# Attention and two feed-forward blocks on one core: plain float32 scores for batch 0, and a Float64 conversion that shifts on ScalarE

## The chip, the cores and the metric

The program runs on one core of a Trainium2 chip. The metric is the device time of one execution in microseconds (us). Five engines work side by side, each on its own queue, in order: TensorE (PE, with its weight loads as PEld), VectorE (DVE), ScalarE (ACT), GpSimd (POOL) and SyncE (SP), which here only issues DMAs.

## The reference

Attention with rotary embedding over 4 batches, 8 heads, 576 positions, 64 features; then a layer norm with a two-layer feed-forward block (512 to 2048 to 512) and a residual; then a gated block with a causal convolution of 5 taps.

```python
q_rot, k_rot = rotate(q), rotate(k)
scores = scale * q_rot @ k_rot.T
attn = softmax(scores)
x = attn @ v                                  # (4, 576, 512) after the heads are joined
xn = layer_norm(x) * g_ln
x = x + relu(xn @ w_ch1) @ w_ch2
gate = sigmoid(causal_conv5(x, conv_w))
out = (gate * (x @ w_val)) @ w_out
```

The weights arrive as Float64 and are converted on the chip.

## The kernel before

**Order.** Every piece of work is a step with an engine, an assumed duration, a rank, the steps that it waits for and the buffers that it takes. A planner (class `Plan`) plays these steps through once while the program is built and so fixes the order in which each engine gets its instructions. On the chip each engine takes them strictly in that order. A changed duration or dependency can therefore move work anywhere in the program.

**Attention.** A part is a batch and a pair of heads (and, in batches 0 and 1, a range of rows of q). For each part SP loads k (576 columns) and q (`load`); DVE multiplies by the rotary table (`mul`, L308) and adds the two halves (`add`, L312). Then the rotated value is split: ACT rounds it to float32r, the reduced float32 that TensorE takes in one pass (`hi`, L326), and DVE writes the remainder (`lo`, L330). A score tile has 128 rows by 576 columns in two halves of 288; `a_scores` (L443) adds three products of halves (high by high, high by low, low by high). Two heads sit in the two halves of the partitions and go as a pair: 12 matmuls. A last tile per part (its "lead", with the 64 left-over rows of both heads put in a block-diagonal `qd`) takes 6. Behind a score tile come the row maximum (DVE, L448), the exponential (ACT, L454), a split into two float16 (ACT L460, DVE L465), a transposing DMA to `pT`, and the products with v (PE, L489 and L492). Two score tiles fit in PSUM at a time. Batch 0 has 16 pairs and 4 leads; its k lies in `kx0`, which batch 1 uses again.

**Weights.** Each of 16 blocks of `w_ch1` and `w_ch2` (1024 columns of Float64, 1 MB) is loaded, then turned into float32 by `Conv`: ACT makes the upper bits from the upper word (`p1`, L586), DVE shifts the result left by 3 (L590) and then ors in the lower word, shifted right by 29 (L591; both in `p2`). PE forms a bound of the column norms (L607); from it come scales, and the float32 block is split into two float16 (ACT L645, DVE L648). The first feed-forward product (L745, `f1`) needs the blocks of `w_ch1`; the second (L773, `f2`) those of `w_ch2`, which are split last.

**Tail.** The gated block works on pairs of row tiles, nine in all: the residual output (DVE L777), a byte shuffle (DVE L868), a transposing DMA, a copy back (DVE L880), a float32r split (ACT L888, DVE L893), the gate (DVE L908 among others), four groups of value products (PE L921, 12 matmuls each), the product with the gate and its split (DVE L926, ACT L932, DVE L936), and two groups of output products (PE L948, 12 each).

Of the kernel before, what the change touches and what calls it, by code (L numbers as in the profile page):

```python
# [11 lines left out]
I32 = mybir.dt.int32  # L12
ACTF = mybir.ActivationFunctionType
# [140 lines left out]
def kernel(ctx: ExitStack, tc: tile.TileContext, qk, v, g_ln, w_ch1, w_ch2, w_val, conv_w, w_out, rope, eye, out):  # L154
    nc = tc.nc
# [19 lines left out]
    plan = Plan(dict(raw0=RAW, raw=RAW, qx=2, qs=QS, kx0=1, kx1=1, kx2=1, kx3=1, kq=KQ, qd=1, vt0=2, vt=1, vh=NP, sv=4, vb=2, vm=2, ss=2, so=1, nmx=4, p32=2, p16=P16, pT=PT,  # L175
# [16 lines left out]

    kx0 = xpool.tile([128, NP, 2, S], F32R, name="kx0", tag="x1")
# [44 lines left out]
    c_q = plan.step(POOL, 0.4, -999, lambda: nc.gpsimd.memset(qd.bitcast(F32), 0.0))  # L238
# [48 lines left out]
    def plan_prep(p):  # L287
# [17 lines left out]
        def mul(n):  # L305
            a = st["r", n]
            t = (rope_sb[:, :, q0:q1], rope_sb)[n]
            nc.vector.tensor_tensor(out=a, in0=a, in1=t, op=ALU.mult)  # L308

        def add(n):  # L310
            a = st["r", n]
            nc.vector.tensor_tensor(out=a[:, 0], in0=a[:, 0], in1=a[:, 1], op=ALU.add)  # L312

        def hi(n):
# [4 lines left out]
            elif n:  # L319
                st["x"][1] = kx0[:, pr]  # L320
            elif p >= NP:
                st["x"][0] = ap_q.tile([128, 2, QX], F32R, name="qs", tag="qs", bufs=QS)[:, :, 0:nq]
                st["x"][1] = prep[base[p]]["x"][1]
            else:
                st["x"][0] = pool.tile([128, 2, nq], F32R, name="qx", tag="qx", bufs=2)
# [6 lines left out]
        def diag():  # L332
            c = ts[0][1] - q0
            for h in range(2):
                sl = slice(64 * h, 64 * h + 64)
                nc.scalar.copy(out=qd[sl, :, sl], in_=st["x"][0].bitcast(F32)[sl, :, c:c + 64])

        ready = [bufs[base[p]]["k"]] if two else []
        for n in ((0,) if two else (1, 0)):
# [5 lines left out]
            x = plan.step(DVE, dve(w), r, lambda n=n: add(n), after=[x], uses=[bf["raw", n]])  # L345
            takes = []
            if n:
                takes = [Buf("kq" if b > 1 else f"kx{pr}")]
                bf["kq"] = takes[0]
            elif b < 2:  # L350
                takes = [Buf("qs" if p >= NP else "qx")]
                bf["q"] = takes[0]
            else:
                bf["q"] = bf["kq"]
            uses = [bf["raw", n]] + ([bf["q"]] if not n and not takes else [])
# [16 lines left out]
        if ts[0][0] is None:  # L372
            bf["qd"] = Buf("qd")
# [55 lines left out]
    def a_scores(i):  # L429
# [4 lines left out]
        if h is None:  # L434
            todo = [(slice(0, 128), qd)]
# [93 lines left out]
    for i in range(NS):  # L529
# [3 lines left out]
        if h != 1:  # L533
            ne = 1 if h is None else 2
            ss = [Buf("ss") for _ in range(ne)]
            x = plan.step(PE, 0.85 if h is None else 1.08, R_SC + i, lambda i=i: a_scores(i), after=bf["ready"] + ([bf["dg"]] if h is None else []), takes=ss,
# [4 lines left out]
            if b < 2:  # L541
# [42 lines left out]

# [469 lines left out]
```

## Time and profile before

| | |
|---|---|
| median of 3 runs | 786.35 us (785.13 to 787.8) |
| the profiled execution | 786.84 us |
| its span, first to last instruction | 785.0 us |
| PE, DVE, ACT busy | 88%, 82%, 56% of the span |
| mean granted clock of TensorE | 0.948 of 2.4 GHz |

The difference between the profiled execution and its span, 1.84 us, lies around the program. Shares over the whole span are averages over stages with different limits, so the stages are read one by one below.

### The profile page before, as it was taken

Reading aid. Unit: us, or ns where it says so; the run is one execution under the profiler, and the core shown is the slowest. Engines: PE = TensorE matmul, PEld = TensorE weight load, DVE = VectorE, ACT = ScalarE, POOL = GpSimd, SP = SyncE. Lnnn points to the kernel's source line nnn. Section 1 sums busy time; section 2 is a strip of 40 time slices with the busy share of each in tenths; the row PEclk is TensorE's granted clock in tenths of the full one; section 3 lists DMA queues with packets and bytes.
Section 4 is the critical chain, followed back from the end, with each engine's and each line's share of the span. In section 5 each row is a group of like instructions: output and inputs, shape, how many; then the busy total and the mean of one; then the engine's idle time right before and its main releaser. Section 6 shows DMA issues by size and latency. Waiting matters only on the chain.

```text
span 785.0 us, 19308 instructions
## 1 busy us (share of the span) xinstructions
PE 688.6 (88%) x8001; PEld 541.5 (69%) x8001; DVE 640.5 (82%) x1302; ACT 440.8 (56%) x773; POOL 16.4 (2%) x39
## 2 busy tenths in 40 slices
PE   1344868868999999999999999999999999999967
PEld 1233757744678776767687878777787888888746
DVE  6989989999989999997899978677799997664225
ACT  5755655787776556776767666554444443343113
POOL 0000000000000000000000000000000000000000
PEclk9985877778999999999999999999999999999988
DMA  8996489855888898788789687657424321010100
GB/s 308 247 313 141 79 215 281 188 129 133 127 144 145 169 186 163 135 162 170 125 163 179 110 137 128 114 109 217 85 52 81 54 68 42 28 41 29 41 14 28
DMA packets 231736, 103.62 MB, mean 132 GB/s; under 512 B 210784, under 2 KB 218976, under 8 KB 231648
## 3 DMA queue, kind: packets, MB, share of 16 engines
q1 hardware_dynamic: 231648, 102.39, 61.4%
q8 instruction: 63, 1.03, 0.5%
q14 instruction: 25, 0.20, 0.1%
HBM read 45.73 MB, written 4.72 MB: 64 GB/s over the span
## 4 chain that ended last, share of the span: by engine, by line
PE 58%; DVE 23%; DMA 10%; ACT 5%; issue 4%; SPq 0%; ACTq 0%; DVEq 0%
PE acc L773 17%; PE hp L745 16%; DMA pT<-p 8%; PE po L948 6%; PE sc L443 6%; PE pv L921 5%; PE ov L489 4%; DVE p L465 3%; DVE nmx L448 3%; DVE raw L308 2%; DVE gt L908 2%; PE ov L492 2%; DVE wall L648 2%; ACT p L454 1%; DMA raw<-in_qk_dram 1%
## 5 line engine op out<-in xcount | busy, mean ns | idle before, releaser
L745 PE MATMUL hp<-xT,wall 128*128 128x128 f16 x3456 | 209.6, 222 | 2.2 <-DVE wall L648 2.2
L745 PEld LDWEIGHTS <-wall 128*128 128x128 f16 x3456 | 199.4, 99 | 7.2 <-DVE wall L648 2.5
L773 PE MATMUL acc<-wall,hh 128*128 128x512 f16 x544 | 162.9, 381 | 0.0
L454 ACT ACTIVATE p<-sc,nmx 128x576 f32<-128x576 f32 x144 | 105.3, 735 | 87.5 <-DVE nmx L448 86.4
L465 DVE SCALAR_TENSOR_TENSOR p<-p,p 128x576 f16<-128x576 f32 x144 | 107.2, 752 | 22.4 <-ACT p L460 21.4
L489 PE MATMUL ov<-vh,pT 128*128 128x65 f16 (+1 forms) x1296 | 97.4, 203 | 29.2 <-DMA pT<-p 23.0
L489 PEld LDWEIGHTS <-pT 128*128 128x128 f16 x1296 | 81.2, 101 | 47.2 <-DMA pT<-p 32.7
L448 DVE TENSOR_REDUCE nmx<-sc 128x1 f32<-128x576 f32 x144 | 104.8, 748 | 3.1 <-PE sc L443 3.0
L773 PE MATMUL acc<-wall,hl 128*128 128x512 f16 x272 | 103.4, 380 | 0.0
L460 ACT ACTIVATE p<-p 128x576 f16<-128x576 f32 x144 | 97.4, 681 | 4.4 <-DMA pT<-p 1.6
L773 PEld LDWEIGHTS <-hh 128*128 128x128 f16 x544 | 48.9, 98 | 50.9 <-issue 2.2
L908 DVE SCALAR_TENSOR_TENSOR gt<-xT,cw,gt 128x256 f32<-128x256 f32 (+4 forms) x192 | 72.1, 413 | 5.5 <-ACT gt L899 2.9
L763 DVE SCALAR_TENSOR_TENSOR hl<-hp,hh 128x512 f16<-128x512 f32 x68 | 46.6, 685 | 30.9 <-ACT hh L757 30.9
L492 PE MATMUL ov<-vl,pT 128*128 128x64 f16 (+1 forms) x720 | 71.0, 203 | 0.0
L757 ACT ACTIVATE hh<-hp 128x512 f16<-128x512 f32 x68 | 40.2, 591 | 45.6 <-PE hp L745 45.2
L492 PEld LDWEIGHTS <-pT 128*128 128x128 f16 x720 | 54.8, 102 | 3.4
L921 PE MATMUL pv<-xh,wvh 128*128 128x256 f32 x144 | 45.2, 314 | 6.5 <-ACT xh L888 6.5
L308 DVE TENSOR_TENSOR raw<-raw,rope_sb 128x1152 f32<-128x1152 f32 (+2 forms) x56 | 46.8, 835 | 3.6 <-DMA raw<-in_qk_dram 3.6
L773 PEld LDWEIGHTS <-hl 128*128 128x128 f16 x272 | 26.7, 98 | 32.6 <-issue 0.6
L443 PE MATMUL sc<-kx,qs 64*128 64x288 f32 x336 | 38.2, 344 | 12.0 <-ACT p L454 12.0
L948 PE MATMUL po<-woh,gv 128*128 128x512 f32 x144 | 47.3, 399 | 0.4 <-DVE gv L936 0.4
L921 PE MATMUL pv<-xl,wvh 128*128 128x256 f32 x144 | 41.8, 290 | 1.1 <-DVE xl L893 1.1
(118 smaller groups left out, 944.4 us busy)
## 6 DMA issues: line engine op xcount, KB each, us to landing
raw<-in_qk_dram SPq DMA_DIRECT2D x24, 576.0 KB, 4.5
wall<-in_moe_w_ch_dram SPq DMA_DIRECT2D x8, 1024.0 KB, 6.2
kk<-in_moe_w_ch_dram SPq DMA_DIRECT2D x8, 1024.0 KB, 6.1
vt<-in_v_dram SPq DMA_DIRECT2D x16, 320.0 KB, 3.2
out_dram<-x SPq DMA_DIRECT2D x18, 256.0 KB, 2.0
raw<-in_qk_dram SPq DMA_DIRECT2D x24, 128.0 KB, 2.8
pT<-p SPq DMA_TRANSPOSE x144, 3.4
r<-in_moe_w_val_dram SPq DMA_DIRECT2D x4, 512.0 KB, 4.9
```

The source lines that it names most:

```text
L443: nc.tensor.matmul(live[i + e][:, half, 0:HS], lw[rows, a], xk[rows, k, half * HS:(half + 1) * HS], start=(n == 0), stop=(n == 2))
L448: nc.vector.tensor_reduce(out=nmx, in_=sc[:, :, 0:HS], axis=AX.XY, op=ALU.max, negate=True)
L454: nc.scalar.activation(out=p32.rearrange("p (e n) -> p e n", e=2), in_=sc[:, :, 0:HS], func=ACTF.Exp, bias=nmx)
L460: nc.scalar.activation(out=p16[:, 0], in_=p32, func=ACTF.Copy, scale=P_SCALE)
L465: nc.vector.scalar_tensor_tensor(out=p16[:, 1], in0=p32, scalar=P_SCALE, in1=p16[:, 0], op0=ALU.mult, op1=ALU.subtract)
L489: nc.tensor.matmul(o, pT[:, c], vh[:, 2 * c + hs:2 * c + hs + nh], start=(c == 0), stop=(c == 8))
L492: nc.tensor.matmul(o[..., 0:D], pT[:, c], vl[:, 2 * c + hs:2 * c + hs + nh], start=False, stop=False)
L745: nc.tensor.matmul(hp[:, j], w1[:, u, wl * 512 + o:wl * 512 + o + 128], xT[:, xl * KD + c], start=(i == 0), stop=(i == 3 * KD - 1))
L773: nc.tensor.matmul(st["acc"], lw[:, j], w2[:, f + j, lo * 512:lo * 512 + 512], start=(f + j == 0 and i == 0), stop=(f + j == KF - 1 and i ...
L908: nc.vector.scalar_tensor_tensor(out=gt[:, c0:c1], in0=xT[:, c, HALO + c0 - s:HALO + c1 - s], scalar=col(KT - 1 - s, c), in1=gt[:, c0:c1], ...
L921: nc.tensor.matmul(pv, lw[:, d, c * 128:(c + 1) * 128], rx[:, d], start=(n == 0), stop=(n == 3 * KD - 1))
L948: nc.tensor.matmul(po, lw[:, d, sl], rx[:, d, :], start=(n == 0), stop=(n == 3 * KD - 1))
```

## The change

There are four edits.

1. **Scores of batch 0.** Its rotated q and k are not split any more. `add` writes float32 straight into tiles of its own (`kf` for k, `qx` or `qf` for q, `qdf` for the block-diagonal lead), the factor 0.125 moves into `mul` for q, and `hi` and `lo` fall away. `a_scores` multiplies float32 by float32, one matmul per half and head: 4 per pair, 2 per lead. Batch 1's k no longer shares a buffer with batch 0's.
2. **Conversion.** A new step on ACT, `p0`, reads the top 16 bits of each lower word, scales and rounds them (that is the shift right by 29) and writes the integer over the lower word. DVE's two instructions become one: shift left by 3 and or.
3. **DMA scratch.** The program is built with 1 KB of it, which leaves room for `kf`.
4. **Order.** The planner's durations follow these edits, and so the whole order is planned anew.

```diff
-            nc.vector.tensor_tensor(out=a, in0=a, in1=t, op=ALU.mult)
+            if b == 0 and n == 0:
+                nc.vector.scalar_tensor_tensor(out=a, in0=a, scalar=0.125, in1=t, op0=ALU.mult, op1=ALU.mult)
+            else:
+                nc.vector.tensor_tensor(out=a, in0=a, in1=t, op=ALU.mult)
 
         def add(n):
             a = st["r", n]
-            nc.vector.tensor_tensor(out=a[:, 0], in0=a[:, 0], in1=a[:, 1], op=ALU.add)
-
-        def hi(n):
+            o = a[:, 0]
+            if b == 0:
+                home(n)
+                o = st["x"][n][:, 0]
+            nc.vector.tensor_tensor(out=o, in0=a[:, 0], in1=a[:, 1], op=ALU.add)
...
+        if parts[p][0] == 0:
+            for half in range(2):
+                for e, (rows, lw) in enumerate(todo):
+                    nc.tensor.matmul(live[i + e][:, half, 0:HS], lw[rows, 0], xk[rows, 0, half * HS:(half + 1) * HS], start=True, stop=True)
+            return
...
-            x = plan.step(PE, 0.85 if h is None else 1.08, R_SC + i, lambda i=i: a_scores(i), after=bf["ready"] + ([bf["dg"]] if h is None else []), takes=ss,
+            x = plan.step(PE, (1.1 if h is None else 1.45) if b == 0 else 0.85 if h is None else 1.08, R_SC + i, lambda i=i: a_scores(i), after=bf["ready"] + ([bf["dg"]] if h is None else []), takes=ss,
...
+        def p0(self):
+            low = self.raw[:, :, 0]
+            top = self.scratch[:, 0:2 * self.n].bitcast(U16).rearrange("p (n four) -> p n four", four=4)[:, :, 1]
+            nc.scalar.activation(out=low, in_=top, func=ACTF.Copy, scale=2.0 ** -13, bias=-4095.5 / 8192)
...
-            nc.vector.tensor_scalar(out=ai, in0=ai, scalar1=3, scalar2=None, op0=ALU.logical_shift_left)
-            nc.vector.scalar_tensor_tensor(out=ai, in0=self.raw[:, :, 0], scalar=29, in1=ai, op0=ALU.logical_shift_right, op1=ALU.bitwise_or)
+            nc.vector.scalar_tensor_tensor(out=ai, in0=ai, scalar=3, in1=self.raw[:, :, 0], op0=ALU.logical_shift_left, op1=ALU.bitwise_or)
...
-                x = p2s[w, g] = plan.step(DVE, dve(1024) + 0.73, r, c.p2, after=[x], uses=[raw] if w else [])
+                x = plan.step(ACT, act(1024) + 0.05, r, c.p0, after=[x], uses=[raw] if w else [])
+                x = p2s[w, g] = plan.step(DVE, dve(1024) + 0.07, r, c.p2, after=[x], uses=[raw] if w else [])
...
-    nc = _bacc.Bacc("TRN2", target_bir_lowering=False, num_devices=1)
+    nc = _bacc.Bacc("TRN2", target_bir_lowering=False, num_devices=1, dynamic_dma_scratch_size=1024)
```

What stands where, at three places. First DVE near the first weight block of the program, before (`p` is the split of a probability tile, `raw` and `qx` are q on its way to the scores, `wall` the weight block):

```order
L312 TENSOR_TENSOR raw<-raw 128x128
L465 SCALAR_TENSOR_TENSOR p_226<-p_217,p_226 128x576
L330 SCALAR_TENSOR_TENSOR qx<-raw,qx 128x128
L590 TENSOR_SCALAR wall<-wall 128x1024
L591 SCALAR_TENSOR_TENSOR wall<-wall 128x1024
L308 TENSOR_TENSOR raw<-raw,rope_sb 128x1152
L394 TENSOR_REDUCE vm<-hp 128x1
```

And now (L322 is the add, L312 the product with the table, L478 the row maximum):

```order
L312 SCALAR_TENSOR_TENSOR raw<-raw,rope_sb 128x2x128
L322 TENSOR_TENSOR qf<-raw 128x128
L625 SCALAR_TENSOR_TENSOR wall<-wall 128x1024
L478 TENSOR_REDUCE nmx<-sc 128x1
L625 SCALAR_TENSOR_TENSOR wall<-wall 128x1024
L312 SCALAR_TENSOR_TENSOR raw<-raw,rope_sb 128x2x128
L322 TENSOR_TENSOR qf<-raw 128x128
```

The shift (L590) and the remainder (L330) are gone from DVE, and the first weight block comes behind four score maxima where it came behind two. Counted to the last weight split (L648 before, L682 now), DVE had 345 instructions and has 300: the 16 shifts and the 20 remainders of batch 0 are gone, and 9 instructions of attention (one product with the table, one scaling of v with its five rows of DVE, one normalisation with three) stand behind that point now.

Second, PE at the first two pairs of scores, before:

```order
L390 LDWEIGHTS vb
L390 MATMUL hp<-ident,vb 128x128
L443 MATMUL sc<-kx_68,qx 128x288 x12
L390 LDWEIGHTS vb
L390 MATMUL hp<-ident,vb 128x128
L443 MATMUL sc<-kx_68,qx 128x288 x12
```

And now:

```order
L415 LDWEIGHTS vb
L415 MATMUL hp<-ident,vb 128x128
L468 MATMUL sc<-kf,qx 128x288 x4
L415 LDWEIGHTS vb
L415 MATMUL hp<-ident,vb 128x128
L468 MATMUL sc<-kf,qx 128x288 x4
```

Twelve float32r matmuls of a pair became four of float32, at the same place. Up to the first second-layer product (L773 before, L808 now), PE has 15 pairs and 4 leads of batch 0 before, and 15 pairs and 3 leads now.

Third, DVE at the end of the program, around the residual output of the last row tile, before (L777 is that output, L880 and L893 the copy and the split of the last pair of row tiles):

```order
L926 TENSOR_TENSOR gt<-pv,gt 128x256
L936 TENSOR_TENSOR gv_11605<-gt,gv_11604 128x256
L763 SCALAR_TENSOR_TENSOR hl<-hp,hh 128x512
L880 COPY xT_11739<-tx 128x2x4x128
L882 COPY xT_11739<-xT_11032 128x4x4
L763 SCALAR_TENSOR_TENSOR hl<-hp,hh 128x512 x3
L777 SCALAR_TENSOR_TENSOR x_4517<-acc,scl,x_4517 128x512
L868 COPY rope_sb<-x_4517 128x1024
L880 COPY xT_11739<-tx 128x2x4x128
L893 TENSOR_TENSOR xl_11972<-xT_11739,xh_11971 128x1024
```

And now (L812 the residual output, L962 and L972 the last value group of the pair of row tiles before the last, L916 and L929 the copy and the split of the last):

```order
L962 TENSOR_TENSOR gt<-pv,gt 128x256
L972 TENSOR_TENSOR gv_11692<-gt,gv_11691 128x256
L812 SCALAR_TENSOR_TENSOR x_4504<-acc,scl,x_4504 128x512
L904 COPY rope_sb<-x_4504 128x1024
L962 TENSOR_TENSOR gt<-pv,gt 128x256
L972 TENSOR_TENSOR gv_11692<-gt,gv_11691 128x256
L916 COPY xT_11416<-tx 128x2x4x128
L929 TENSOR_TENSOR xl_11788<-xT_11416,xh_11787 128x1024
```

The last value group of the eighth pair of row tiles, with its DVE work, has moved behind the last feed-forward tile. On PE nothing stood between the last second-layer product and the last pair's four value groups before; now one value group (12 matmuls) and two output groups (24 matmuls) of the eighth pair stand there.

## Rows read from the trace of the kernel before

**Rows 1.** The page: span, and two of its rows of 40 slices.
```profile
span 785.0 us, 19308 instructions
...
PE   1344868868999999999999999999999999999967
...
PEclk9985877778999999999999999999999999999988
```

**Rows 2.** Windows by stage: length, engines' busy time, PEclk, DMA share, GB/s.
```profile
0.00:96.00 96.00, 44.37 (x495) 36.94 (x495) 83.18 (x185) 59.16 (x94) 1.80 (x10) 0.87 0.78 220
96.00:164.00 68.00, 50.91 (x663) 45.20 (x663) 63.04 (x128) 43.45 (x74) 1.85 (x4) 0.75 0.90 216
164.00:188.00 24.00, 19.37 (x115) 10.51 (x116) 23.25 (x37) 21.56 (x35) 0.18 (x1) 0.79 0.48 122
...
205.00:740.00 535.00, 524.96 (x6341) 414.77 (x6339) 439.55 (x893) 295.11 (x531) 11.41 (x22) 1.00 0.60 115
...
759.00:785.00 26.00, 14.74 (x73) 12.14 (x72) 13.56 (x28) 7.01 (x15) 0.00 (x0) 0.80 0.11 31
```

**Rows 3.** Windows: the stretch to the last weight split.
```profile
0.00:187.00 187.00, 113.65 (x1268) 92.20 (x1269) 168.48 (x346) 124.17 (x202) 3.83 (x15) 0.82 0.79 207
```

**Rows 4.** Waits of DVE in 0 to 187 us, the longest group.
```profile
DVE gmax L248 <- PE gt L245: 4.6, 1, 4.6
```

**Rows 5.** Groups by line and shape, 0 to 210 us: busy us, mean ns.
```profile
L590 DVE TENSOR_SCALAR wall<-wall 128x1024 int32<-128x1024 int32 x16 | 11.0, 685 | 0.0
...
L591 DVE SCALAR_TENSOR_TENSOR wall<-kk,wall 128x1024 int32<-128x1024 int32 x8 | 9.8, 1225 | 0.3
...
L586 ACT ACTIVATE wall<-kk 128x1024 f32<-128x1024 f32 x8 | 9.1, 1148 | 2.8 <-DVE wall L591 2.2 <-DMA kk<-in_moe_w_ch_dram 0.5
...
L330 DVE SCALAR_TENSOR_TENSOR kx<-raw,kx 128x576 fp32r<-128x576 f32 x8 | 6.0, 749 | 0.0
...
L326 ACT ACTIVATE kx<-raw 128x576 fp32r<-128x576 f32 x8 | 5.4, 675 | 4.0 <-DVE raw L312 3.9
...
L330 DVE SCALAR_TENSOR_TENSOR qs<-raw,qs 128x192 fp32r<-128x192 f32 x8 | 2.8, 349 | 0.0
...
L330 DVE SCALAR_TENSOR_TENSOR qs<-raw,qs 128x128 fp32r<-128x128 f32 x8 | 2.3, 283 | 0.0
...
L330 DVE SCALAR_TENSOR_TENSOR qx<-raw,qx 128x128 fp32r<-128x128 f32 x4 | 1.1, 286 | 0.1
```

**Rows 6.** Timeline of DVE: start us, us; a conversion, and the last weight split.
```profile
154.12 0.75 DVE L330 SCALAR_TENSOR_TENSOR kx<-raw,kx 128x576 fp32r<-128x576 f32 x1
154.79 0.69 DVE L590 TENSOR_SCALAR wall<-wall 128x1024 int32<-128x1024 int32 x1
155.51 1.22 DVE L591 SCALAR_TENSOR_TENSOR wall<-kk,wall 128x1024 int32<-128x1024 int32 x1
...
185.78 1.28 DVE L648 SCALAR_TENSOR_TENSOR wall<-wall,s 128x1024 f16<-128x1024 f32 x1 [0.44 <-ACT wall L645]
```

**Rows 7.** Timeline of PE: score pairs early and late, and a lead.
```profile
36.01 1.80 PE L443 MATMUL sc<-kx,qx 64*128 64x288 f32 x11 [1.81 <-ACT p L454]
...
204.07 1.07 PE L443 MATMUL sc<-kx,qs 64*128 64x288 f32 x12
...
208.23 1.06 PE L443 MATMUL sc<-kx,qd 128*128 128x288 f32 x6
```

**Rows 8.** Timeline of PE at the end of the program.
```profile
758.80 0.38 PE L773 MATMUL acc<-wall,hl 128*128 128x512 f16 x1
...
766.93 0.58 PE L921 MATMUL pv<-xl,wvh 128*128 128x256 f32 x1 [0.68 <-DVE xl L893]
```

**Rows 9.** Chain that ended last: start us, us, what.
```profile
717.33 5.61 PE po L948 x24
722.93 1.41 PE pv L921 x12
...
776.42 4.90 PE po L948 x19
```

More of the change, by code (lines that the diff above doesn't have):

```diff
@@ L12 @@
 I32 = mybir.dt.int32
+U16 = mybir.dt.uint16
 ACTF = mybir.ActivationFunctionType
@@ L191 @@
     xs = [xpool.tile([128, NT // 2, DM], F32, name="x0")]
+    kf = const.tile([128, NP, S], F32, name="kf")
+    qdf = const.tile([128, 128], F32, name="qdf")
     kx0 = xpool.tile([128, NP, 2, S], F32R, name="kx0", tag="x1")
@@ L237 @@
     c_c = plan.step(SP, 1.0, -500, consts, size=40000)
-    c_q = plan.step(POOL, 0.4, -999, lambda: nc.gpsimd.memset(qd.bitcast(F32), 0.0))
+    c_q = plan.step(POOL, 0.4, -999, lambda: (nc.gpsimd.memset(qd.bitcast(F32), 0.0), nc.gpsimd.memset(qdf, 0.0)))
     c_g = plan.step(ACT, 0.2, -999, lambda: nc.scalar.activation(out=gab, in_=g_sb, func=ACTF.Abs), after=[c_c])
@@ L344, in plan_prep @@
             x = plan.step(DVE, dve(2 * w), r, lambda n=n: mul(n), after=[x, c_r], uses=[bf["raw", n]])
-            x = plan.step(DVE, dve(w), r, lambda n=n: add(n), after=[x], uses=[bf["raw", n]])
             takes = []
             if n:
-                takes = [Buf("kq" if b > 1 else f"kx{pr}")]
+                takes = [Buf("kq" if b > 1 else f"kx{pr}" if b else f"kf{pr}")]
                 bf["kq"] = takes[0]
             elif b < 2:
-                takes = [Buf("qs" if p >= NP else "qx")]
+                takes = [Buf("qx" if p < NP else "qs" if b else "qf")]
                 bf["q"] = takes[0]
@@ L354, in plan_prep @@
                 bf["q"] = bf["kq"]
+            if b == 0:
+                y = plan.step(DVE, dve(w), r, lambda n=n: add(n), after=[x], takes=takes, uses=[bf["raw", n]], row="hi")
+                ready.append(y)
+                bf["k" if n else "ql"] = y
+                if p < NP:
+                    early.append(y)
+                attention.append(y)
+                continue
+            x = plan.step(DVE, dve(w), r, lambda n=n: add(n), after=[x], uses=[bf["raw", n]])
             uses = [bf["raw", n]] + ([bf["q"]] if not n and not takes else [])
@@ L540 @@
                 early.append(x)
-            if b < 2:
+            if b == 1:
                 kx_users.append(x)
@@ L851 @@
         x = plan.step(ACT, act(n), r, lambda st=st: st["c"].p1(), after=[x], takes=[tb], uses=[rb], row="tw1")
-        x = plan.step(DVE, dve(n) + n / 1920 + 0.07, r, lambda st=st: st["c"].p2(), after=[x], uses=[rb, tb])
+        x = plan.step(ACT, act(n), r, lambda st=st: st["c"].p0(), after=[x], uses=[rb])
+        x = plan.step(DVE, dve(n), r, lambda st=st: st["c"].p2(), after=[x], uses=[rb, tb])
         if nm == "cw":
```

21 lines of the change are left out of this document (14 added, 7 removed).

## The prediction, made before the change was run

> **What bounds the kernel now.** I read the page's slices first: PE is full from about 200 us to 745 us, and in the first quarter it is not, at a clock that is often below full [rows 1]. The windows then say what fills each stretch [rows 2]. From 205 to 740 us PE is busy 524.96 of 535 us at full clock, so that stretch is as long as PE's work. Before it DVE is the busiest engine: 83.18 of 96 us, 63.04 of 68 us, 23.25 of 24 us, while PE has 44.37 of 96 and 50.91 of 68. In all DVE is busy 168.48 of the 187 us that end with the last weight split [rows 3, 6]. The list of its waits says that the 18.5 us of idle time have no one cause; the longest is 4.6 us at the start [rows 4]. Not before the weights of the second layer are split can PE run second-layer products freely, so an instruction taken off DVE ahead of 187 us brings the full stretch of PE forward by its length. The end has a limit of its own: after the last second-layer product, which ends at 758.80 + 0.38 = 759.2 us, PE waits until 766.93 us for the last row tile to come through DVE, a transposing DMA and ACT, and does one matmul in between [rows 8]. From there the gate on DVE holds back the last output products, which go on at 776.42 us [rows 9].
>
> **The change, part by part.**
>
> *Shift off DVE.* Sixteen shifts of 1024 columns take 685 ns each [rows 5]; the or that follows starts 155.51 - 154.79 = 0.72 us after the shift does [rows 6]. 16 x 0.72 = 11.5 us. The or itself stays an instruction with two tensor inputs and one strided read, so I keep its 1225 ns.
>
> *Remainders off DVE.* Batch 0 has 4 of k (749 ns), 4 of q in `qx` (286), 8 of 128 columns (283) and 4 of 192 (349) [rows 5]: 3.0 + 1.1 + 2.3 + 1.4 = 7.8 us. An independent instruction starts about 0.07 us before the one ahead of it ends (154.12 + 0.75 against 154.79) [rows 6], so in line these 20 cost 7.8 - 1.4 = 6.4 us. `mul` and `add` have the same sizes as before, and I cost their new forms at nothing: both already read two tensors.
>
> *Moved behind the last weight split.* By the order, one product with the table, one scaling of v and one normalisation, 9 instructions. They are as wide as 1152, 640 and 128 columns; at the rate of the widest remainder (749 ns for 576) the first two alone are near 1.5 and 0.8 us. I take 3.4 us for the nine. They come back where DVE has room: 439.55 of 535 us are busy there [rows 2].
>
> DVE's rows to that point thus shrink by 11.5 + 6.4 + 3.4 = 21.3 us.
>
> *New work on ACT.* `p0` is not in the trace. The nearest row is `p1`, also 1024 columns with a stride of 8 bytes: 1148 ns [rows 5]. Below nothing is excluded; at best it is as short as one of 576 columns (675 ns), at worst, if reading 2 bytes and writing 4 at a stride each cost a full pass, 2.3 us. I take 1.15. Sixteen add 18.4 us; the four copies of k that go give back 2.7 [rows 5], the sixteen shorter ones of q more. ACT then has less than 124.17 + 15.7 = 140 us in some 167, less dense than DVE is now. So I cost it at no more than a later start: load, `p1`, `p0`, or is 1.15 - 0.72 = 0.4 us longer per block, and five times a scale waits for the last block of a group. 5 x 0.4 = 2 us, half of it hidden by score work on DVE: 1 us. If that cover were gone it would be 2, and with `p0` at 2.3 us 5 x 1.6 = 8. The nine conversions of the tail lie in the full stretch of PE and are hidden by it.
>
> *Scores on PE.* No row shows a float32 matmul. The 12 matmuls of a float32r pair take 1.8 us early in the program and 1.07 us later [rows 7]. If a float32 matmul were one such pass, 4 of them would take 0.6 us early on. At the other end, if the two heads no longer ran side by side and each matmul took four passes, 16 passes at the pace of a lead (1.06 us for 6) [rows 7] are 2.8 us, and early on 1.80 / 1.07 times that, 4.8 us. I take the nearest row, 1.8 us, no change. What hides a longer time: PE is idle for 164 - 95.3 = 68.7 us in the first two windows [rows 2], and only one pair and one lead of batch 0 come behind the first second-layer product. The Trainium skill ("FP8 and Floating Point Precision", section TensorE Precision Notes) says that true float32 takes four passes through the array; by it a pair would be 16 passes for 12, about 2.4 us early in the program, and the sum below would grow by some 0.7 us, a third of 1.07 and of 1.06 us for the pair and the lead that come late. No run here shows it yet.
>
> *DMA.* The same bytes have to move sooner. In 96 to 164 us the DMA engines are busy for 0.90 x 68 = 61 us [rows 2]. Of the 21.3 us, nearly 10 fall in this window (eight shifts, six remainders, part of what moved), which would shorten it to 58. I let it shrink to 61 and give back 3 us. The smaller scratch I cost at nothing: if it made more work on POOL, POOL, busy 3.83 of 187 us [rows 3], would hide it; should it slow the transfers themselves, that is the second rival below.
>
> *The end.* One value group (1.41 us) and two output groups (5.61 us) [rows 9] of the eighth pair now stand behind the last second-layer product. They fit in the 7.7 us in which PE waits [rows 8], and the DVE chain that sets the end is not lengthened: their product with the gate runs while the transposing DMA is under way. The last second-layer product itself then comes 1.41 + 5.61 = 7.0 us sooner, and so does the end.
>
> **Sum.** 785.0 - 21.3 + 1 + 3 - 7.0 = 760.7 us of span. With the 1.84 us around it the profiled execution would take 762.5; before, it stood 0.5 us above the median, so from a span to a median it is 1.3 us, and I predict a median of **762 us**.
>
> **Rivals.**
>
> *The end is not filled* (if the output groups wait for their last value group until the gap is over): the 7.0 us are lost, 769 us. Against it: only the last 3 of 12 matmuls of an output group need that value group.
>
> *Transfers or ACT hold the first stretch.* For it: DMA's share of 0.78 and 0.90 [rows 2] over 164 us is 136 us of work. If 0.87 is all that it can sustain, these windows last 156 us, where DVE's rows, 19.3 of the 21.3 us being ahead of 164 us, would let them shrink to 145; the gain falls to 8 + 2 = 10 us, and the time is 785.0 - 10 + 1 - 7.0 + 1.3 = 770 us. `p0` at 2.3 us ends near 762 - 1 + 8 = 769 us. Against it: DVE hardly ever waits for a DMA today.
>
> *No net change.* The new order may put instructions so that the gain is lost in waits on other queues, or a planned duration may be off by enough to do so; 21.3 + 7.0 us would have to go. I see no place that costs this much: 786 us.
>
> *Slower: the score pair holds up DVE.* DVE's queue is in order, so whatever stands behind a row maximum waits with it. If a float32 pair takes 4.8 us, the maxima of each of the 16 pairs come 3.0 us late: 48 us, 36 if a quarter is hidden, and the time is 762 + 36 = 798 us. It decides from (786.35 + 2.4 - 762) / 16 = 1.7 us lost per pair. Against it: DVE has other rows between the maxima of two pairs, (168.48 - 21.3) / 18 = 8 us of work for each pair if a lead counts as half of one.
>
> **How the numbers follow.** Chances: as forecast (755 to 767) 0.60; end not filled 0.10; transfers or ACT 0.18; no net change 0.06; slower 0.06. 0.3% of the time, 2.4 us, is about what a measurement of this kernel can tell from no change. Faster is 0.60 + 0.10 + 0.18 = 0.88, the same 0.06, slower 0.06. The range takes in the first three cases with their bounds: at the low end no give-back and a faster float32 pair (785.0 - 21.3 - 7.0 + 1.3 = 758, less 3 us for idle time of PE between 205 and 740 us that the new order may close), at the high end the transfer case with a share of 0.84, which leaves 2 + 2 us of gain: 755 to 776 us.
>
> **What would show it.** Right: the last weight split ends near 170 us instead of 187; no shift of 685 ns is left; `p0` stands at about 1.15 us; PE's full stretch begins some 17 us sooner; and the wait of PE between the last second-layer product and the last value groups is under 1 us. Wrong: DVE waits for score matmuls or for ACT by more than 4 us in all over what it waits now; a pair of float32 scores over 3.5 us; windows before 150 us with the DMA share above 1 and DVE idle.

## The result, and the profile after

The changed kernel takes 765.57 us (median of 4 runs, 764.5 to 767.51); the kernel before, timed beside it, takes 786.01 us (4 runs, 785.13 to 787.8). The ratio is 0.974, 95% interval 0.9713 to 0.9767: faster, 3.6 us above the predicted 762 and inside the range. The profiled execution took 765.1 us, its span is 763.3 us, 2.6 us above the 760.7 of the sum. The other 1.0 us lies between span and median: 2.3 us here, 1.3 in the prediction.

The page after, with the rows that answer to [rows 1] (a slice is now 19.1 us):

```profile
span 763.3 us, 19105 instructions
...
PE   2575766789999999999999989999999999999996
...
PEclk9977989889999999999999999999999999999999
```

PE is full from the tenth slice (172 us) on, before from the eleventh (196 us), and the last two slices of the clock row, 8 before, are at 9. Line numbers have moved: the or is L625 (it was L591), `p1` L621 (L586), the new `p0` L618, the second-layer split L682 (L648), second-layer products L808 (L773), value groups L957 (L921), output groups L984 (L948); batch 0's scores are L468, the others L473 (L443).

The windows of the changed kernel (columns as in [rows 2]); the first ends with the last weight split, as [rows 3] did, and the last with the last second-layer products:

```profile
0.00:172.40 172.40, 109.58 (x1176) 80.30 (x1177) 148.43 (x301) 127.89 (x188) 3.77 (x16) 0.88 0.91 221
100.00:120.00 20.00, 15.01 (x204) 12.14 (x201) 17.79 (x37) 12.87 (x22) 0.73 (x1) 0.83 1.23 231
120.00:140.00 20.00, 13.89 (x215) 11.70 (x213) 14.66 (x28) 13.48 (x21) 0.55 (x1) 1.00 0.99 231
128.00:134.00 6.00, 3.35 (x46) 2.47 (x44) 3.39 (x8) 5.33 (x9) 0.00 (x0) 1.00 1.24 240
172.40:738.00 565.60, 554.44 (x6655) 433.76 (x6654) 459.25 (x929) 318.02 (x573) 12.57 (x24) 1.00 0.62 114
```

The same two 20 us windows in the kernel before:

```profile
100.00:120.00 20.00, 12.45 (x167) 10.56 (x164) 17.86 (x38) 10.44 (x17) 0.95 (x1) 0.76 0.89 240
120.00:140.00 20.00, 18.45 (x274) 17.17 (x274) 18.98 (x34) 13.38 (x23) 0.00 (x0) 0.84 1.08 280
```

Up to the last weight split DVE now has 301 instructions and 148.43 us of work, against 346 and 168.48 [rows 3]: 45 rows and 20.05 us less. The stretch shrank by 187.06 - 172.4 = 14.7 us only, so DVE's idle time in it rose from 18.5 to 24.0 us. Most of the new idle time lies in 120 to 140 us, where DVE works 14.66 of 20 us against 18.98 before, right behind a window in which the DMA share is 1.23. Within it, in 128 to 134 us, the share is 1.24 and DVE works 3.39 of 6 us. The list of DVE's waits (0 to 172 us: us in total, times, longest) and its timeline name what came late (`ov` are the products with v, `rd` belongs to the normalisation behind them, `gmax` is a maximum taken once at the start, `raw` is a piece of q or k as it was loaded, `hp` at L415 is a small product for the scaling of v and `vm` the maximum that DVE takes of it):

```profile
DVE rd L537 <- PE ov L519: 6.7, 7, 2.6
DVE gmax L251 <- PE gt L248: 5.0, 1, 5.0
DVE raw L314 <- DMA raw<-in_qk_dram: 2.8, 2, 2.5
DVE vm L419 <- PE hp L415: 1.8, 3, 1.0
```

In the kernel before (0 to 187 us) the two that grew most were:

```profile
DVE rd L507 <- PE ov L489: 2.9, 4, 1.7
DVE raw L308 <- DMA raw<-in_qk_dram: 0.5, 1, 0.5
```

And in the timeline of DVE after:

```profile
132.24 0.56 DVE L314 TENSOR_TENSOR raw<-raw,rope_sb 128x384 f32<-128x384 f32 x1 [2.51 <-DMA raw<-in_qk_dram]
...
171.13 1.28 DVE L682 SCALAR_TENSOR_TENSOR wall<-wall,s 128x1024 f16<-128x1024 f32 x1
```

The view of the DMA queues in 100 to 142 us of the changed kernel, and below it of the kernel before (share of 16 engines' time; then issues, KB each, median us from issue to landing):

```profile
q1 hardware_dynamic: 16640, 9.43, 109.3%
...
raw<-in_qk_dram SPq DMA_DIRECT2D x2, 192.0 KB, 7.5
pT<-p SPq DMA_TRANSPOSE x11, 6.1
```

```profile
q1 hardware_dynamic: 16496, 11.02, 99.0%
...
raw<-in_qk_dram SPq DMA_DIRECT2D x4, 192.0 KB, 3.2
...
pT<-p SPq DMA_TRANSPOSE x10, 5.5
```

A piece of q and k of 192 KB takes 7.5 us to land where it took 3.2 in the same stretch of time, a transpose of p 6.1 where it took 5.5. DVE's longest wait for `ov` is one step removed from this: the products `ov` wait for transposes, and DVE's normalisation waits for `ov`. The list of PE's waits in 100 to 142 us has this after the change, and no such row before:

```profile
PE ov L519 <- DMA pT<-p: 7.3, 4, 3.1
```

The new and the shortened instructions, by line and shape (busy us, mean ns):

```profile
L618 ACT ACTIVATE wall<-wall 128x1024 int32<-128x1024 uint16 x8 | 9.1, 1135 | 0.0
...
L625 DVE SCALAR_TENSOR_TENSOR wall<-wall 128x1024 int32<-128x1024 int32 x8 | 9.7, 1214 | 0.0
```

No 685 ns shift is left. The score products of batch 0 in the timeline of PE, an early pair, a pair at 84 us, a lead and the last pair [rows 7]:

```profile
10.07 2.29 PE L468 MATMUL sc<-kf,qx 64*128 64x288 f32 x8
...
84.52 1.24 PE L468 MATMUL sc<-kf,qf 64*128 64x288 f32 x8
...
160.70 1.19 PE L468 MATMUL sc<-kf,qdf 128*128 128x288 f32 x4
...
166.17 1.66 PE L468 MATMUL sc<-kf,qf 64*128 64x288 f32 x8
```

The end, in the timeline of PE [rows 8]:

```profile
737.06 0.38 PE L808 MATMUL acc<-wall,hl 128*128 128x512 f16 x1
...
744.07 0.39 PE L984 MATMUL po<-woh,gv 128*128 128x512 f32 x1
745.25 0.38 PE L957 MATMUL pv<-xl,wvh 128*128 128x256 f32 x1 [0.67 <-DVE xl L929]
...
754.74 0.73 PE L984 MATMUL po<-woh,gv 128*128 128x512 f32 x2 [1.44 <-DVE gv L972]
```

Behind the last second-layer product PE now does a value group and two output groups, until 744.46 us, and waits 0.67 us where a gap of some 7 us was. The last second-layer product ends 25.8 us before the end of the span, as before. So the 21.7 us of span come from two places: 14.7 from the stretch to the last weight split, and 7.0 from the one between that and the last second-layer product (572.1 us before, 565.1 after), which has handed its last 7 us of value and output products to the gap.

### The profile page after: what moved, and what is told of

Its sections match the earlier page's. It is cut to its first block, busy times and chain, and to the rows that moved or that the text cites. A ratio compares the mean times of both kernels' runs of the same rounds, so it can differ in the third digit from the quotient of the medians.

```text
span 763.3 us, 19105 instructions
## 1 busy us (share of the span) xinstructions
PE 683.1 (89%) x7929; PEld 529.0 (69%) x7929; DVE 621.5 (81%) x1257; ACT 454.4 (60%) x778; POOL 16.3 (2%) x40
## 4 chain that ended last, share of the span: by engine, by line
PE 57%; DVE 22%; DMA 13%; ACT 5%; issue 3%; SPq 1%; ACTq 0%; DVEq 0%
PE acc L808 17%; PE hp L780 16%; DMA pT<-p 9%; PE pv L957 6%; PE po L984 6%; PE sc L473 4%; DVE p L495 3%; PE ov L519 3%; DVE nmx L478 3%; PE sc L468 2%; DMA vt<-in_v_dram 2%; DVE wall L682 2%; DVE raw L314 2%; PE ov L522 2%; DVE wall L625 1%
## 5 line engine op out<-in xcount | busy, mean ns | idle before, releaser
L780 PE MATMUL hp<-xT,wall 128*128 128x128 f16 x3456 | 206.0, 220 | 1.6 <-DVE wall L682 1.6
L780 PEld LDWEIGHTS <-wall 128*128 128x128 f16 x3456 | 196.6, 98 | 7.3 <-DVE wall L682 1.8
L808 PE MATMUL acc<-wall,hh 128*128 128x512 f16 x544 | 162.1, 380 | 0.4 <-DVE x L812 0.4
L495 DVE SCALAR_TENSOR_TENSOR p<-p,p 128x576 f16<-128x576 f32 x144 | 107.6, 753 | 27.5 <-ACT p L490 27.2
L519 PE MATMUL ov<-vh,pT 128*128 128x65 f16 (+1 forms) x1296 | 93.7, 200 | 27.3 <-DMA pT<-p 17.1
L519 PEld LDWEIGHTS <-pT 128*128 128x128 f16 x1296 | 79.2, 100 | 45.5 <-DMA pT<-p 28.3
L478 DVE TENSOR_REDUCE nmx<-sc 128x1 f32<-128x576 f32 x144 | 105.0, 750 | 4.1 <-PE sc L473 3.6
L808 PE MATMUL acc<-wall,hl 128*128 128x512 f16 x272 | 103.1, 379 | 0.0
L808 PEld LDWEIGHTS <-hh 128*128 128x128 f16 x544 | 48.6, 98 | 51.3 <-issue 2.3
L522 PE MATMUL ov<-vl,pT 128*128 128x64 f16 (+1 forms) x720 | 68.9, 200 | 0.0
L522 PEld LDWEIGHTS <-pT 128*128 128x128 f16 x720 | 53.4, 100 | 4.2 <-issue 0.3
L808 PEld LDWEIGHTS <-hl 128*128 128x128 f16 x272 | 26.6, 98 | 32.9 <-DVE hl L798 1.1
L984 PE MATMUL po<-woh,gv 128*128 128x512 f32 x144 | 47.7, 400 | 1.8 <-DVE gv L972 1.4
L957 PE MATMUL pv<-xh,wvh 128*128 128x256 f32 x144 | 44.1, 307 | 0.0
L314 DVE TENSOR_TENSOR raw<-raw,rope_sb 128x1152 f32<-128x1152 f32 (+2 forms) x40 | 39.6, 991 | 4.3 <-DMA raw<-in_qk_dram 4.3
L957 PE MATMUL pv<-xl,wvh 128*128 128x256 f32 x144 | 40.6, 282 | 0.7 <-DVE xl L929 0.7
L957 PE MATMUL pv<-xh,wvl 128*128 128x256 f32 x144 | 40.5, 281 | 0.0
```

The lines of the kernel that those rows point to most:

```text
L478: nc.vector.tensor_reduce(out=nmx, in_=sc[:, :, 0:HS], axis=AX.XY, op=ALU.max, negate=True)
L495: nc.vector.scalar_tensor_tensor(out=p16[:, 1], in0=p32, scalar=P_SCALE, in1=p16[:, 0], op0=ALU.mult, op1=ALU.subtract)
L519: nc.tensor.matmul(o, pT[:, c], vh[:, 2 * c + hs:2 * c + hs + nh], start=(c == 0), stop=(c == 8))
L522: nc.tensor.matmul(o[..., 0:D], pT[:, c], vl[:, 2 * c + hs:2 * c + hs + nh], start=False, stop=False)
L780: nc.tensor.matmul(hp[:, j], w1[:, u, wl * 512 + o:wl * 512 + o + 128], xT[:, xl * KD + c], start=(i == 0), stop=(i == 3 * KD - 1))
L808: nc.tensor.matmul(st["acc"], lw[:, j], w2[:, f + j, lo * 512:lo * 512 + 512], start=(f + j == 0 and i == 0), stop=(f + j == KF - 1 and i ...
```

## The experiments

Twelve kernels were run. Each is compared with the kernel before on the same chip (785.0 us in the first group of four, 785.35 and 785.73 in the others); ratios are to that, with a 95% interval. For their stages I use three readings of each profile: the end of the last weight split, the length from there to the end of the last second-layer product ("middle"), and the rest ("end"). Before these are 187.1, 572.1 and 25.8 us, after 172.4, 565.1 and 25.8.

**The conversion alone** is the kernel before with `p0`, the new `p2` and their steps in the plan; scores as before.

```
+        def p0(self):
+            low = self.raw[:, :, 0]
...
-            nc.vector.tensor_scalar(out=ai, in0=ai, scalar1=3, scalar2=None, op0=ALU.logical_shift_left)
-            nc.vector.scalar_tensor_tensor(out=ai, in0=self.raw[:, :, 0], scalar=29, in1=ai, op0=ALU.logical_shift_right, op1=ALU.bitwise_or)
+            nc.vector.scalar_tensor_tensor(out=ai, in0=ai, scalar=3, in1=self.raw[:, :, 0], op0=ALU.logical_shift_left, op1=ALU.bitwise_or)
...
+                x = plan.step(ACT, act(1024) + 0.05, r, c.p0, after=[x], uses=[raw] if w else [])
...
```

> The kernel before with the conversion alone changed (shift of the lower words on ACT), order planned anew. By its order DVE has 329 rows to the last weight split instead of 345: the 16 shifts are gone and nothing else moved. Its order also has the last value group of the eighth pair of row tiles behind the last feed-forward tile. My theory (DVE's rows set the first stretch, transfers give a part back, the end is a separate 7.0 us): -11.5 + 2.5 for the first stretch, -7 for the end, about 770 us, ratio 0.979. Rival (the whole gain needs the float32 scores, the conversion only moves the load from DVE to ACT): only the end, 779 us, 0.991.

Measured: 772.6 us, ratio 0.9846 (0.9812 to 0.9879); stages 177.3, 566.3, 25.8. The ratio lies between the two that were expected, 0.979 and 0.991, and its interval holds neither. By the two profiles 9.8 us come from the first stretch and 5.8 from the middle, as its planned order fills the end as well; that is 3 us more than the 12 us of the medians, which is what single profiles scatter.

**The scores alone** is the changed kernel with those lines taken back.

> The changed kernel with the conversion of before (DVE shifts), order planned anew. DVE has 309 rows to the last weight split instead of 345, and the order also fills the end. My theory: -6.4 us for the 20 remainders and about -4 for score work that stands behind that point now, less 2 for transfers and for the longer float32 matmuls, and -7 for the end: about 771 us, ratio 0.981. Rival (float32 pairs hold up DVE): the first stretch gains nothing, 779 us, 0.991.

Measured: 784.23 us, ratio 0.9975 (0.9949 to 1.0001): next to nothing, outside both expectations. Its stages are 172.9, 581.8 and 27.3: the last split comes as early as in the full change, and the gain is lost behind it. Its windows show where:

```profile
187.00:426.00 239.00, 227.37 (x3090) 174.92 (x3089) 202.20 (x392) 155.03 (x270) 5.43 (x14) 1.00 0.78 146
426.00:450.00 24.00, 17.99 (x185) 14.17 (x184) 21.74 (x44) 13.08 (x24) 3.48 (x5) 0.72 0.66 143
```

In the second window PE waits for three things in a row, and after the first of them its granted clock is at the lower level, 0.50, from 432 to 445 us. The list of PE's waits from 424 to 446 us, and the chain that ended last around it:

```profile
PE ov L519 <- DVE p L495: 1.9, 1, 1.9
PE sc L473 <- ACT p L484: 1.6, 1, 1.6
PE hp L775 <- DMA xT<-x: 1.6, 1, 1.6
```

```profile
419.19 5.16 DMA pT<-p
...
425.14 0.76 DVE p L495
...
425.90 1.33 DVE nmx L478 x2
427.24 1.33 DVE kq L344 x2
428.57 0.66 DVE x L807
429.23 0.14 DVE rd L537
```

A transpose lands 5.16 us after its issue; behind the `p` that comes of it DVE has two maxima, two remainders of k and a second-layer sum to do before it gets to the normalisation `rd`, and PE waits for what follows. The list puts PE's first wait down to the `p` (DVE L495) that ended at 430.71 us, but a `p` gets to PE only through a transposing DMA. The kernel has a single buffer for `ov`, which the normalisation has to empty before the next `ov` may begin, and ACT's share of that ended at the same 430.71 us:

```profile
430.08 0.63 ACT L549 ACTIVATE x<-ov,rd 64x64 f32<-64x64 f32 x2 [0.18 <-DVE x L542]
```

So it is the normalisation that PE waits for, and it stands behind the same five DVE rows. The next two experiments ask whether this belongs to the edit or to the order that the planner made of it.

**The scores alone, in the order of the full change**: the changed kernel with `p0` left empty and the two old DVE instructions inside `p2`. The edits are those of the run above; the plan does not know of it.

```
         def p0(self):
...
-            nc.scalar.activation(out=low, in_=top, func=ACTF.Copy, scale=2.0 ** -13, bias=-4095.5 / 8192)
+            pass
...
-            nc.vector.scalar_tensor_tensor(out=ai, in0=ai, scalar=3, in1=self.raw[:, :, 0], op0=ALU.logical_shift_left, op1=ALU.bitwise_or)
+            nc.vector.tensor_scalar(out=ai, in0=ai, scalar1=3, scalar2=None, op0=ALU.logical_shift_left)
+            nc.vector.scalar_tensor_tensor(out=ai, in0=self.raw[:, :, 0], scalar=29, in1=ai, op0=ALU.logical_shift_right, op1=ALU.bitwise_or)
```

> The change with ACT's lower-word step left empty and the two DVE instructions of the kernel before (shift, then or) back in the conversion, all of it in the planned order of the changed kernel: the same edits as the run with the scores alone (784.2 us), in another order; on DVE the order is that of the changed kernel with 25 shift rows added. Theory (the scores-alone run lost 16.7 us after the last weight split to its own planned order: 8 us more idle TensorE between 180 and 720 us and a granted clock of 0.5 from 432 to 445 us): no such stretch here, so the time from the last split to the last second-layer product is 564 to 569 us as in the other runs and the end 25.8; the 16 shifts of 685 ns put the last split at 178 to 183.4 us in place of 172.4; time 770 to 776, ratio 0.98 to 0.988. Rival (the shifts that are left on DVE cost the middle stretch, whatever the order): the middle stretch takes about 580 us again and the time is 784 to 792, ratio 0.998 or more.

Measured: 771.37 us, ratio 0.9822 (0.9793 to 0.985); stages 176.9, 566.6, 25.8. The same two windows:

```profile
187.00:426.00 239.00, 230.97 (x3146) 178.85 (x3144) 210.84 (x411) 159.11 (x279) 7.42 (x16) 1.00 0.83 150
426.00:450.00 24.00, 23.55 (x309) 17.72 (x308) 23.29 (x46) 16.15 (x28) 2.00 (x3) 1.00 0.74 136
```

The theory holds for the middle and the time: the same instructions in another order are 0.9975 - 0.9822 = 0.0153 of the time faster, 12 us. Only the last split came sooner than expected, at 176.9 us in place of 178 to 183.4. PE's idle time in these 263 us is 8.5 us instead of 17.6, and no clock is lost, where by an estimate from the window's clock 24 x (1 - 0.72) = 6.7 us were; 9.1 + 6.7 = 15.8 us answers to the difference of the middle stretches, 581.8 - 566.6 = 15.2.

**The scores alone, with one planner cost 0.07 us lower** (`dve(1024) + 0.66` for 0.73).

> The run with the scores alone, with one number of the planner changed: the cost entered for the conversion's DVE step of a 1024-element chunk 0.07 us lower (dve(1024) + 0.66 in place of 0.73). The instructions are the same but for a handful, in another order. Theory (the order lost the gain): the middle stretch is below 575 us and the time between 765 and 779, ratio 0.975 to 0.992. Rival (the edit itself brings nothing without the other): 782 to 786 again, ratio 0.995 to 1.001.

Measured: 775.54 us, ratio 0.9876 (0.9847 to 0.9906); stages 166.9, 580.9, 25.8. The time is where the theory put it, for another reason than it gave: the last split came 6 us earlier, and the middle stretch, expected below 575 us, was as long as in the first run with the scores alone. Its windows show the same fall of the clock:

```profile
426.00:450.00 24.00, 20.50 (x256) 17.86 (x257) 21.76 (x43) 15.47 (x25) 2.54 (x4) 0.73 0.67 117
```

The chain shows that the planner had laid the same piece of order here once more, the two maxima, the two remainders and the sum ahead of the normalisation, and here the list of PE's waits (415 to 450 us) names the normalisation itself:

```profile
PE ov L519 <- ACT x L549: 1.9, 1, 1.9
```

**The end held back** is the changed kernel in which the last second-layer product has to wait for the eighth pair's output groups, so that these do not come in the gap.

```
+        last_f2 = f2s
...
+            if m == NB - 2:
+                last_f2.deps.append(x)
```

> The changed kernel with one more dependency: the last second-layer product waits for the output groups of the eighth pair of row tiles, as the order before had it. My theory (7.0 us of PE's work lie in a wait that is there anyway): +7.0 us, 772.5 us, ratio 0.983. Rival (the gain at the end is only another place for the same wait, or all of it comes from the first stretch): no change, 765.5 us, 0.974.

Measured: 771.03 us, ratio 0.9831 (0.9788 to 0.9875); stages 169.3, 573.9, 25.8. The timeline of PE has the gap again:

```profile
742.80 0.38 PE L808 MATMUL acc<-wall,hl 128*128 128x512 f16 x1
749.68 0.58 PE L958 MATMUL pv<-xh,wvh 128*128 128x256 f32 x1 [6.50 <-ACT xh L925]
```

As the theory had it, the 7.0 us are gone.

**The end filled in the kernel before**: no other edit, only the eighth pair's last value group and its output groups tied behind the last second-layer product.

```
+        last_f2 = f2s
...
-            x = plan.step(PE, 1.45, R_VAL + m, lambda m=m, c=c: val(m, c), after=[h, l] + w3["wv"] + ([gate_order] if c else []), takes=[pv], uses=[x3], row="val")
+            x = plan.step(PE, 1.45, R_VAL + m, lambda m=m, c=c: val(m, c), after=[h, l] + w3["wv"] + ([gate_order] if c else []) + ([last_f2] if m == NB - 2 and c == KD - 1 else []), takes=[pv], uses=[x3], row="val")
...
-            x = plan.step(PE, 2.85, R_PROJ + m, lambda m=m, s=s: proj(m, s), after=lasts + w3["wo"], takes=[po], uses=[gv], row="proj")
+            x = plan.step(PE, 2.85, R_PROJ + m, lambda m=m, s=s: proj(m, s), after=lasts + w3["wo"] + ([last_f2] if m == NB - 2 else []), takes=[po], uses=[gv], row="proj")
```

> The kernel before, with none of the edits, but with the last value group and both output groups of the eighth pair of row tiles made to wait for the last second-layer product. My theory: -7.0 us, 779 us, ratio 0.991. Rival (the end needs the edits): no change, 786 us, 1.000.

Measured: 777.83 us, ratio 0.9915 (0.9885 to 0.9945); stages 185.1, 564.8, 25.8. The wait before the last value groups is gone, with the conversion and the scores untouched:

```profile
757.69 0.39 PE L922 MATMUL pv<-xl,wvh 128*128 128x256 f32 x1 [0.63 <-DVE xl L894]
```

**Half of the bytes loaded**: each weight block's load brings half of its row blocks; the other halves of the buffers are cleared once at the start. DVE's order is that of the changed kernel.

```
...
-            nc.sync.dma_start(out=raw.rearrange("p (a n) -> p a n", a=self.src.shape[1]), in_=self.src)
+            h = max(1, self.src.shape[1] // 2)
+            nc.sync.dma_start(out=raw.rearrange("p (a n) -> p a n", a=self.src.shape[1])[:, 0:h], in_=self.src[:, 0:h])
```

> The changed kernel with the 16 weight loads halved (the second half of each block is zeros set once), in the same order: 8.4 MB less to move in the first 140 us. My theory (DVE's 24 us of idle time to the last weight split, 5.4 more than before, are mostly late transfers): 3 to 5 us of it come back, 761.5 us, ratio 0.969. Rival (the idle time is waits on PE and ACT): no change, 765.5 us, 0.974.

Measured: 758.63 us, ratio 0.9656 (0.963 to 0.9682), past what the theory expected; stages 166.5, 565.7, 25.9. The windows, DVE's wait for `ov` up to 166 us, and PE's wait for transposes in 100 to 142 us:

```profile
0.00:166.50 166.50, 112.67 (x1176) 83.45 (x1177) 148.32 (x301) 127.22 (x188) 8.22 (x21) 0.90 0.77 179
...
120.00:140.00 20.00, 16.81 (x255) 14.11 (x252) 19.62 (x38) 18.22 (x31) 0.73 (x2) 1.00 0.90 191
```

```profile
DVE rd L537 <- PE ov L519: 2.7, 4, 0.9
```

```profile
PE ov L519 <- DMA pT<-p: 0.7, 2, 0.4
```

DVE's work to the last split is the same 148.3 us, its idle time 18.2 instead of 24.0, and 120 to 140 us is full again (19.62 of 20). The wait for `ov` falls from 6.7 to 2.7 us and the one for `raw` is no longer among the seven longest. In 100 to 142 us a 192 KB piece of q and k now lands after 3.9 us and a transpose of p after 4.2. The kernel before was not run with half of the bytes.

**`p0` left empty, and `p0` twice.** DVE's order is that of the changed kernel in both. In the first the or becomes an and, which takes the unconverted lower word as a mask.

```
-            nc.scalar.activation(out=low, in_=top, func=ACTF.Copy, scale=2.0 ** -13, bias=-4095.5 / 8192)
+            pass
...
-            nc.vector.scalar_tensor_tensor(out=ai, in0=ai, scalar=3, in1=self.raw[:, :, 0], op0=ALU.logical_shift_left, op1=ALU.bitwise_or)
+            nc.vector.scalar_tensor_tensor(out=ai, in0=ai, scalar=3, in1=self.raw[:, :, 0], op0=ALU.logical_shift_left, op1=ALU.bitwise_and)
```

The second kernel has the line of `p0` twice:

```
             nc.scalar.activation(out=low, in_=top, func=ACTF.Copy, scale=2.0 ** -13, bias=-4095.5 / 8192)
+            nc.scalar.activation(out=low, in_=top, func=ACTF.Copy, scale=2.0 ** -13, bias=-4095.5 / 8192)
```

> The changed kernel without the new ACT instruction, in the same order; the lower words go in unshifted and with an and in place of the or, so the weights are wrong. ACT loses 25 instructions, 18 us of them in the first stretch. My theory (ACT costs a later start of a block, some 1 us in all): 763.5 to 765.5 us, ratio 0.973. Rival (ACT now holds the first stretch): 6 to 7 us faster, 759 us, 0.966.

> The changed kernel with the new ACT instruction done twice, in the same order, so that the low bits of the weights are wrong: 18 us more of ACT in the first stretch. My theory: blocks come 1.1 us later, five times on the way, partly hidden: 2 to 6 us slower, 768 to 771 us, ratio 0.979. Rival (ACT is the bound): 15 us or more slower, 780 us, 0.993.

Measured: 764.84 us, ratio 0.9737 (0.9711 to 0.9763), without `p0`; 772.46 us, ratio 0.983 (0.9808 to 0.9852), with two. The stages are 171.0, 568.5, 25.9 and 176.9, 566.0, 27.2. The first `p0` costs nothing that can be measured, as the theory had it; a second one costs about 7 us, a little more than the 2 to 6 expected and far from the 15 of the rival.

**Scores of batch 0 in one pass**: the new tiles `kf`, `qf`, `qx` and `qdf` as float32r instead of float32, so that each product is one matmul of lower precision. DVE's order is that of the changed kernel.

```
-    kf = const.tile([128, NP, S], F32, name="kf")
-    qdf = const.tile([128, 128], F32, name="qdf")
+    kf = const.tile([128, NP, S], F32R, name="kf")
+    qdf = const.tile([128, 128], F32R, name="qdf")
...
```

> The changed kernel with batch 0's rotated q and k rounded to float32r, one product and no split, in the same order: its scores keep only the high halves. It takes the extra time of float32 off PE and nothing off DVE or ACT. My theory (PE has idle time there): the first stretch gets shorter by at most 1.5 us, 764 to 765.5 us, ratio 0.973. Rival (float32 scores hold up DVE's row maxima): a pair falls from about 2.3 to about 0.7 us early on, 16 x 1.6 = 26 us of waits, of which a third or more shows: 757 us or less, 0.963.

Measured: 762.05 us, ratio 0.9701 (0.9678 to 0.9724), between theory (0.973) and rival (0.963), nearer to the theory. A first pair in the timeline of PE:

```profile
9.86 0.85 PE L468 MATMUL sc<-kf,qx 64*128 64x288 f32 x4 [0.19 <-DVE qx L322]
```

**One pass, and the planner told so**: the kernel above with 0.45 us as the planned length of a score step of batch 0, in place of 1.1 and 1.45.

> The change with batch 0's score products in one pass on f32r tiles (762.0 us in the run before) and the planner told so: 0.45 us for a score step of batch 0 in place of 1.1 and 1.45. The order becomes another. Theory (the order of the first stretch is set by DVE, not by what the planner thinks TensorE needs): 758 to 767 us, ratio 0.965 to 0.977, no clear gain over 762. Rival (the true costs give a better order): 757 or less, ratio 0.964 or less.

Measured: 767.09 us, ratio 0.9752 (0.971 to 0.9794). The planner's other number gives another order and no gain: at the upper edge of what the theory allowed, and by the ratios 4 us slower than the order made with the longer cost, where the two intervals just overlap.

**The DMA scratch alone**, in the kernel before: `dynamic_dma_scratch_size=1024`.

> The kernel before with the DMA scratch of 1 KB alone. Theory (the setting does nothing for the time and only frees memory): ratio 1.000, between 0.997 and 1.003. Rival (it changes how the DMA queues are served): a difference above 0.5% either way, with another time to landing of the transposes.

Measured: 786.16 us, ratio 0.9999 (0.9979 to 1.0019). The setting does nothing by itself.

## Why the prediction was right, and where it was off

*Rows off DVE: right in number, less than one for one in worth.* The forecast took 21.3 us off DVE ahead of the last split. The trace shows exactly 16 + 20 + 9 = 45 rows less and 20.05 us less work; the gap behind each shift, 0.72 us from its start to the or for 0.685 us of work, makes up some 0.6 us of the rest, and the last 0.7 us are not taken apart. That DVE's rows set this stretch is shown in the other direction too: the 16 shifts put back in the same order move the last split from 172.4 to 176.9 us and the time by 0.9822 - 0.974 = 0.0082, 6.4 us. So of their 11 us about half returns; the rest falls into waits that DVE has anyway, its idle time up to the last split being 17.7 us there instead of 24.0. The prediction's premise, that an instruction taken off DVE brings the full stretch forward by its whole length, is too strong.

*`p0` on ACT: right.* It takes 1.13 us (forecast 1.15), and taking it away changes the ratio by 0.0003, 0.2 us, less than the intervals tell; the 1 us that the sum had for it is not seen. The other bound of that step was tested as well: 8 us were worked out for a `p0` of 2.3 us, and two of them in a row cost 0.983 - 0.974 = 0.009 of the time, 7 us.

*Float32 scores: mis-sized, at little cost.* I took 1.8 us for an early pair, no change; it is 2.29. Later pairs take 1.24 us (at 84 us) to 1.66 us (the last; 1.07 before), and a lead 1.19 (1.06). The Trainium skill ("FP8 and Floating Point Precision", section TensorE Precision Notes) has four passes for true float32; from it came the 2.4 us that the prediction set beside its own value, and the early pair's 2.29 is near it. The other lengths lie on both sides of what 16 passes for 12 give: 1.43 us for a late pair and 1.41 for a lead. Against the same four matmuls in one pass, 0.85 us, the early pair is 2.7 times as long and not four times; the passes themselves are not counted by any record. What the scores cost the whole program can be bounded only: with one pass in place of them all the time falls by 0.974 - 0.9701 = 0.004, 3 us, and the intervals of the two overlap. A part of it can be named. DVE does not wait for the score products themselves, but PE's queue is in order too, and the small product `hp` (L415) stands behind a pair: DVE waits 1.8 us for it, 1.00 and 0.52 us of that behind pairs of 2.28 and 2.92 us near 20 and 28 us, against 0.0 us before and 0.2 with one pass. The prediction looked for such a hold-up at the row maxima only.

*Transfers: right in kind, probably sized too small.* I gave back 3 us to the DMA engines. With half of the weight bytes the time falls by 0.974 - 0.9656 = 0.0084, 6.6 us, with no instruction moved on DVE, the two intervals do not meet, and the waits that go are the ones of 100 to 140 us. That is what the weight bytes cost the changed kernel; how much of it the kernel before paid as well is not shown by the times. What the change added to it is read from the waits: those of DVE for `ov` and `raw` were 3.4 us, became 9.5, and are 3.1 with half of the bytes. In the run with the end held, which has the same order there, they are 5.5 us, so 2 to 6 us were added. The gain in this stretch was 14.7 us in place of 21.3 - 4 = 17.3, where 4 us had been allowed for transfers and `p0` together: 1.25 us of the difference are the work that was not saved, and DVE's idle time rose by 5.5 us in place of 4. These are the 2.6 us by which the span missed, and they are no more than the scatter of the stretch between profiles (below), so the size of the term rests on the times of the run with half of the bytes and not on them. The rival in which transfers hold the whole stretch (a gain of 10 us, 770 us) is refuted, but its sign was there: the prediction named a DMA share above 1 with DVE idle before 150 us as what would speak against it, and 128 to 134 us shows that. The 192 KB pieces of q and k land in 3.9 us when half of the weight bytes are missing, so the weights are among what they collide with; the share of the transposes was not taken apart.

*The end: right.* 7.0 us were forecast. Holding the groups back costs 0.9831 - 0.974 = 0.009, 7 us; filling the gap in the kernel before gives 0.0085, 6.7 us. So a third of the gain comes from neither edit of the title, but from a place in the order that was free to take before.

*No change, or slower: refuted for this order, and nearer than I thought.* The lists of waits have no sign of the slower rival: DVE's waits for score products were 0.9 us before, and after there is no such row among the longest. But I gave 0.06 to a loss of the gain by the new order with the words that I saw no place that costs this much, and the scores alone in the order that the planner makes of them lost 15 us of the middle stretch at such a place, by waits and by the clock. The full change does not have that piece of order. Nothing in the prediction foresaw this; it was luck. Put together, the parts add up: the conversion in its own order 0.0154 and the scores in the order of the full change 0.0178, each with the filled end, less one end of 0.0085, are 0.0247, and the full change measures 0.026.

The stretch to the last split scatters by some 3 us between profiles: the run with the end held has the same order up to the end and splits at 169.3 us, not 172.4, with 20.5 us of idle time on DVE, not 24.0. Differences of that size between single profiles are therefore not read as causes above; the times are.

Of the kernels that load and convert all of the weights, the fastest was the one with batch 0's scores in one pass, 762.05 us, whose products are of lower precision; its distance to the full change is within what the intervals leave open.

## What to carry to other kernels

When an order is planned by costs, a change is two changes, the instructions and the order: run the same edits in a fixed order before you put a price on them, and look at the end of the program for a gap that can be filled without either. Rows taken off the engine that bounds a stretch return their full length only as far as the transfers of that stretch can come sooner; here, with a DMA share of 0.9 in a part of it, half of the weight bytes were worth 6.6 us where the share's own arithmetic gave back 3 for all transfers. When a release is put down to an instruction whose result still has a DMA to go through, look for another that ended at the same moment. A few waits of PE of 1.6 to 1.9 us amid full work were followed in two runs by a fall of the granted clock that cost as much as the idle time or more (by the estimate above 6.7 and 6.5 us in 24, for 6.0 and 3.5 us of idle time), so the clock row of the page belongs to the first look at any run that is slower than its parts.

## What the runs showed of the hardware that was not expected

- A float32 matmul stands in the trace as two records: a pair of 4 matmuls has 8, a lead of 2 has 4, of 426 to 734 ns each by mean.
- In the run with the scores alone PE waited 1.9 and 1.6 us near 430 us; the granted clock stood at 0.50, the 1.2 GHz level, from 432 to 445 us, and rose after PE had worked without a wait from 440.15 us on.
- In 100 to 142 us, with the share of the DMA queue at 109.3%, two loads of 192 KB took 7.5 us (median) from issue to landing, against 3.2 us at 99.0% in the same stretch of time of the kernel before.
